# Fewer, longer scratch reads for the query features, and three moves in the order of work, in an attention-plus-GLU kernel

## The chip, the cores and the metric

The kernel runs on one core of a Trainium2 chip. The metric is the device time of one execution in microseconds (us), the median over several runs. Before the change it is 329.64 us (329.25 to 329.85 in 3 runs). The profile is one execution of the same kernel; its span is 327.9 us.

## What is computed

The inputs are q, k and v of shape (4 batches, 4 heads, 1088 positions, 32), two sketch matrices S1 and S2 of 8 x 32, and three feed-forward weights.

```python
def phi(x):                       # 32 numbers -> 64 features
    a = einsum('rd,bhsd->bhsr', S1, x)      # 8 numbers
    b = einsum('rd,bhsd->bhsr', S2, x)      # 8 numbers
    return outer(a, b)                      # 8 x 8 = 64
kv  = sum over s of phi(k) x v              # 64 x 32 per head
z   = sum over s of phi(k)                  # 64 per head
x   = (phi(q) @ kv) / (phi(q) @ z + 1e-6)   # heads side by side: (4352, 128)
out = (sigmoid(x @ w_gate) * (x @ w_val)) @ w_out    # d_ff = 1536
```

Everything is fp32. The weights arrive as 64-bit numbers whose halves the kernel puts together itself ("narrowing").

## The kernel before

**The feed-forward part is cut into waves.** The 4352 tokens are taken in chunks of 512, and the 1536 hidden columns in 12 blocks of 128. One wave (`w1`, L286) is one block of one chunk: two matmuls into a PSUM tile called wave (gate and value, L295), a sigmoid on ScalarE (sg, L303), and a gating multiply on VectorE (g, L313). The multiply is not emitted at once: `w1` leaves it in `moe["gate"]`, and `glu()` (L322) emits it when the next wave is due. The output matmul for the block (moeout, L255) follows one or two waves later. An fp32 matmul of the program shows as two PE records, so a wave is four records of L295 and two of L255. The wave tiles rotate through two PSUM buffers, which `qcomp` uses as well.

**During the first chunk the weights are still being narrowed.** Each wave of chunk 0 also emits one step each for several blocks (L304 to L308): two VectorE operations (L105, L109), a ScalarE square (L113), a GpSimd add (L114) and a last VectorE operation (L117) that writes the block of w_sb. A wave cannot start before the L117 of its own block.

**The attention part is worked batch by batch between the waves.** The order on TensorE, VectorE, ScalarE and GpSimd is written out by hand: `slot(group, n)` (L327) emits a group of attention work and then n waves. Instructions of one engine run strictly in the order in which they are emitted. Only the SyncE queue, which issues most DMAs, is ordered by the scheduler.

For a batch b: `turn_k` and `turn_q` (L353, L363) transpose k and q on VectorE. `kps` (L376) makes the sketches of k on TensorE and transposes them back on VectorE (kab, L391); `outer` (L397) makes phi(k) on GpSimd; `kv` (L519) sums over positions.

phi(q) is needed in another layout: 64 features on partitions, once for each of two position sets c, and all heads along the free axis. For batches 1 to 3 and for the second half of batch 0 it is built through DRAM. `qcomp` (L455) makes the compact sketches a and b and copies them to SBUF (cq). `spread` (L482) writes cq to a DRAM scratch tile dq and reads it back twice: into QP with each of the 8 rows of a repeated 8 times in place, and into BQ with the 8 rows of b cycled 8 times. `qmult` (L512) multiplies the two on VectorE (L515). Then `den` (L588) and `num` (L621) are the two products of phi(q) on TensorE, `invert` and `divide` finish x on VectorE.

The positions of a batch are in two halves n: `q_chk` gives 8 and 9 blocks of 32, that is 256 and 288 columns for each c. In the scratch tile before, `[c, h, i, r, column]`, one head's row r is 544 columns long (2,176 bytes), so a read covers one head, one c and one of a/b: 4 x 2 x 2 = 16 reads for each call of `spread`. In batch 0 only the second half goes this way (the first is computed directly, L679 to L692); there the 16 reads have rows of 288 columns, 1,152 bytes.

**The order around the change.** After the first wave of chunk 0 (L708), batch 0 goes on with

```python
    slot(q01, 6)                       # qcomp and spread of batch 0's second half, 6 waves
    qmult(0, 1)                        # VectorE, waits for all 16 reads
    slot(lambda: den(0, 1)(), 1)       # TensorE, reads what qmult wrote
    slot(lambda: num(0, 1)(), 1)
    turn_k(1)
    slot(None, 1)
    turn_q(1, 0)
    turn_q(1, 1)
    slot(None, 1)
```

and then each batch from 1 on starts with `begin(b)` (L711): kps, qcomp, spread, outer. When `begin` is called, the gating multiply of the last wave is still pending, so it is emitted after the kab transposes.

Of the kernel before, what the change touches and what calls it, by code (L numbers as in the profile page):

```python
# [8 lines left out]
F32 = mybir.dt.float32  # L9
# [5 lines left out]
MUL = ALU.mult  # L15

P = 128
# [3 lines left out]
def kernel(  # L21
# [12 lines left out]
    nc = tc.nc  # L34

    B, H, S, D = q.shape
    R = S1.shape[0]
# [359 lines left out]
    def outer(b, pi, m0, m1, j0=0, j1=NJK, eng=nc.gpsimd):  # L397
# [8 lines left out]
            op=MUL,  # L406
        )

    def ab(a_of=None, b_of=None, pool_b=None):

        mm = []
        if a_of is not None:
            aps = psm.tile([P, 2, 512], F32, tag="wave", name="aps")
            mm.append((a_of, aps, sa))
        if b_of is not None:
            pool, tag = (ps2, "two") if pool_b is None else pool_b
            bps = pool.tile([P, 2, 512], F32, tag=tag, name="bps")
# [14 lines left out]
        if a_of is not None:  # L432
            w = 32 * q_chk[a_of[2]][1]
            ASB[a_of] = sbA.tile([P, 2, 256], F32, tag="asb", name="asb", bufs=2)
            nc.scalar.copy(out=ASB[a_of][:, :, :w], in_=aps[:, :, :w])
        if b_of is not None:

            def mult():
                bb, pr, n = b_of
                if bb not in QP:  # L440
                    QP[bb] = sbA.tile([P, H, TP * 32], F32, tag="qp", name="qp")
                t0, tn = q_chk[n]
                w = 32 * tn
                nc.vector.tensor_tensor(
                    out=QP[bb][:, 2 * pr : 2 * pr + 2, 32 * t0 : 32 * t0 + w],
                    in0=bps[:, :, :w],
                    in1=ASB[b_of][:, :, :w],
                    op=MUL,
                )

            return mult
# [3 lines left out]
    def qcomp(b, ns, pool):  # L455
        t = pool[0].tile([P, 2, 512], F32, tag=pool[1], name="cqps")
        cq = sbA.tile([P, 2, 288], F32, tag="cq", name="cq", bufs=1)
        for c in range(2):
            for n in ns:
                t0, tn = q_chk[n]  # L460
                g = 2 * n + c
                for pi in range(2):
                    rows = slice(64 * pi, 64 * pi + 64)
                    nc.tensor.matmul(
                        out=t[32 * g : 32 * g + 32, pi, : 32 * tn],
                        lhsT=sk[rows, :],
                        rhs=qT_of[b][rows, t0 : t0 + tn, c, :],
                        start=True,
                        stop=True,
                    )  # L470
        w0, w1 = 32 * q_chk[0][1], 32 * q_chk[1][1]
        if 0 in ns:
            nc.scalar.copy(out=cq[:, :, :w0], in_=t[:, :, :w0])
            nc.scalar.copy(out=cq[64:, :, w0:w1], in_=t[64:, :, w0:w1])
        else:
            nc.scalar.copy(out=cq[64:, :, :w1], in_=t[64:, :, :w1])
        if b not in QP:
            QP[b] = sbA.tile([P, H, TP * 32], F32, tag="qp", name="qp")
        BQ[b] = sbA.tile([P, H, TP * 32], F32, tag="bq", name="bq", bufs=1)
        return cq  # L480

    def spread(b, ns, cq):  # L482
        w = TP * 32
        d = dram.tile([2, H, 2, R, w], F32, tag="dq", name="dq")
        for c in range(2):
            for n in ns:
                t0, tn = q_chk[n]
                g = 2 * n + c
                d0 = d[c, 0, 0, 0, 32 * t0 : 32 * t0 + 32 * tn]
                nc.sync.dma_start(  # L490
                    out=bass.AP(
                        tensor=d0.tensor,
                        offset=d0.offset,
                        ap=[[w, 4 * R], [4 * R * w, 2], [1, 32 * tn]],
                    ),
                    in_=cq[32 * g : 32 * g + 32, :, : 32 * tn],
                )
        w0, w1 = 32 * q_chk[ns[0]][0], 32 * sum(q_chk[ns[-1]])
        for h in range(H):
            for c in range(2):  # L500
                for i, (t, rows) in enumerate(
                    ((QP[b], [[w, R], [0, R]]), (BQ[b], [[0, R], [w, R]]))
                ):
                    d0 = d[c, h, i, 0, w0:w1]
                    nc.sync.dma_start(  # L505
                        out=t[64 * c : 64 * c + 64, h, w0:w1],
                        in_=bass.AP(
                            tensor=d0.tensor, offset=d0.offset, ap=rows + [[1, w1 - w0]]
                        ),
                    )  # L510

    def qmult(b, n):  # L512
        t0, tn = q_chk[n]
        cols = slice(32 * t0, 32 * t0 + 32 * tn)
        nc.vector.tensor_tensor(  # L515
            out=QP[b][:, :, cols], in0=QP[b][:, :, cols], in1=BQ[b][:, :, cols], op=MUL
        )

    def kv(b, j_list, zsum=None):  # L519

# [67 lines left out]
    def den(b, n):  # L588
        t0, tn = q_chk[n]
        w = 32 * tn  # L590
        dps = ps1.tile([P, 512], F32, tag="one", name="dps")
        for h in range(H):
            nc.tensor.matmul(  # L593
                out=dps[32 * h : 32 * h + 32, :w],
                lhsT=zb[b % 2][:, h, :],
                rhs=QP[b][:, h, 32 * t0 : 32 * t0 + w],
                start=True,
                stop=True,
            )

        def invert():

            dT = sbA.tile([P, 9, 32], F32, tag="dT", name="dT")
            nc.vector.transpose(out=dT[:, :tn].rearrange("p t c -> p (t c)"), in_=dps[:, :w])
            rc = sbA.tile([P, 9, 2], F32, tag="rc", name="rc")
            nc.vector.tensor_scalar_add(rc[:, :tn], dT[:, :tn, :2], 1e-6)
            nc.vector.reciprocal(out=rc[:, :tn], in_=rc[:, :tn])

            rb = sbA.tile([P, 9, 2, 32], F32, tag="rb", name="rb")
            r0 = rc[:, :tn]  # L610
            nc.vector.transpose(
                out=rb[:, :tn].rearrange("p t c s -> p (t c s)"),
                in_=bass.AP(
                    tensor=r0.tensor, offset=r0.offset, ap=[list(r0.ap[0]), [1, 2 * tn], [0, 32]]
                ),
            )
            RB[b, n] = rb

        return invert

    def num(b, n):  # L621
        t0, tn = q_chk[n]
        w = 32 * tn
        nps = ps2.tile([P, 2, 512], F32, tag="two", name="nps")
        for h in range(H):
            for c in range(2):
                rows = slice(64 * c, 64 * c + 64)
                nc.tensor.matmul(  # L628
                    out=nps[32 * h : 32 * h + 32, c, :w],
                    lhsT=ND[b][rows, 32 * h : 32 * h + 32],  # L630
                    rhs=QP[b][rows, h, 32 * t0 : 32 * t0 + w],
                    start=True,
                    stop=True,
                )
# [12 lines left out]

    steps = narrow(sr, sr_in, nc.vector) if wide else iter(())
    for _ in range(3):
# [13 lines left out]
        ),  # L663
        op=MUL,
    )
    sk = sk.rearrange("p m n r -> p (m n r)")
    sab = []
    for n, inner in enumerate(([[1, R], [0, R]], [[0, R], [1, R]])):
# [40 lines left out]
    cq = {}  # L709

    def begin(b):  # L711
        kps(b)
        cq[b] = qcomp(b, (0, 1), (psm, "wave"))
        spread(b, (0, 1), cq[b])
        for pi in range(2):
            for m in range(2):
                outer(b, pi, m, m + 1)
# [7 lines left out]
    def q01():  # L725
        spread(0, (1,), qcomp(0, (1,), (ps2, "two")))

    slot(q01, 6)
    qmult(0, 1)
    slot(lambda: den(0, 1)(), 1)  # L730
    slot(lambda: num(0, 1)(), 1)
    turn_k(1)
    slot(None, 1)
    turn_q(1, 0)
    turn_q(1, 1)
    slot(None, 1)
    for b in range(1, B):
        wn = 2 if b == 1 else 3
        load_batch(b + 1)
# [46 lines left out]
```

## Time and profile before

| | busy us | share of the span |
|---|---|---|
| TensorE matmul (PE) | 307.3 | 94% |
| VectorE (DVE) | 140.1 | 43% |
| ScalarE (ACT) | 81.4 | 25% |
| GpSimd (POOL) | 48.6 | 15% |

| group | count | busy us |
|---|---|---|
| wave matmuls, L295 | 432 | 194.2 |
| moeout matmuls, L255 | 216 | 106.6 |
| gating multiply g, L313 | 102 | 69.9 |
| qmult, L515 | 7 | 9.1 |

The DMA engines move 22.92 MB, 70 GB/s on average over the span, from 31,314 packets, of which 25,408 are under 2 KB. There are 64 reads of the scratch (qp<-dq and bq<-dq, 32 each).

How to read it: PE is busy nearly all the time, but "busy" counts a matmul at half clock as well as one at full clock. So the time that TensorE loses is in two places: stretches in which it does nothing, and stretches in which its granted clock (PEclk) is below 1.

### The profile page before, as it was taken

Reading aid. Unit: us, or ns where it says so; the run is one execution under the profiler, and the core shown is the slowest. Engines: PE = TensorE matmul, PEld = TensorE weight load, DVE = VectorE, ACT = ScalarE, POOL = GpSimd, SP = SyncE. Lnnn points to the kernel's source line nnn. Section 1 sums busy time; section 2 is a strip of 40 time slices with the busy share of each in tenths; the row PEclk is TensorE's granted clock in tenths of the full one; section 3 lists DMA queues with packets and bytes.
Section 4 is the critical chain, followed back from the end, with each engine's and each line's share of the span. In section 5 each row is a group of like instructions: output and inputs, shape, how many; then the busy total and the mean of one; then the engine's idle time right before and its main releaser. Section 6 shows DMA issues by size and latency. Waiting matters only on the chain.

```text
span 327.9 us, 3718 instructions
## 1 busy us (share of the span) xinstructions
PE 307.3 (94%) x1394; PEld 137.5 (42%) x1394; DVE 140.1 (43%) x241; ACT 81.4 (25%) x149; POOL 48.6 (15%) x57
## 2 busy tenths in 40 slices
PE   8789649996999899999999999999999999999994
PEld 2423214343433344444343444444444444444683
DVE  4887738631346513335544323455233222322331
ACT  2544503321121322121222221222222222222220
POOL 1435402570000190000003800000000000000000
PEclk9999959999699999999999999999999999999999
DMA  7997460547100145101001450010002000100021
GB/s 183 363 319 225 117 167 1 173 143 203 33 0 0 26 126 136 54 1 31 1 2 30 139 169 2 1 22 12 0 0 32 0 2 0 32 0 0 0 34 17
DMA packets 31314, 22.92 MB, mean 70 GB/s; under 512 B 19904, under 2 KB 25408, under 8 KB 31296
## 3 DMA queue, kind: packets, MB, share of 16 engines
q1 hardware_dynamic: 30464, 22.29, 24.5%
q10 hardware_dynamic: 832, 0.39, 0.6%
q8 instruction: 11, 0.18, 0.2%
q14 instruction: 7, 0.06, 0.1%
HBM read 19.46 MB, written 3.21 MB: 69 GB/s over the span
## 4 chain that ended last, share of the span: by engine, by line
PE 79%; DMA 6%; SPq 6%; DVE 5%; issue 1%; POOL 1%; ACT 1%; ACTq 0%; DVEq 0%; POOLq 0%
PE wave L295 48%; PE moeout L255 25%; SPq L505 6%; DMA dq<-cq 2%; PE dps L593 2%; DMA out_dram<-o_sb 1%; PE nps L628 1%; PE kvz L528 1%; DMA k<-in_k_dram 1%; PE kps L381 1%; DMA bq<-dq 1%; POOL head L114 1%; DVE w_sb L117 1%; DVE qp L515 1%; DVE kab L391 1%
## 5 line engine op out<-in xcount | busy, mean ns | idle before, releaser
L295 PE MATMUL wave<-xT,w_sb 128*128 128x512 f32 (+1 forms) x432 | 194.2, 577 | 2.2 <-DVE g L313 1.1
L313 DVE TENSOR_TENSOR g<-wave,sg 128x512 f32<-128x512 f32 x102 | 69.9, 686 | 129.0 <-ACT sg L303 128.9
L295 PEld LDWEIGHTS wave<-xT,w_sb 128*128 128x128 f32 x432 | 82.2, 192 | 101.2 <-issue 87.1
L303 ACT ACTIVATE sg<-wave 128x512 f32<-128x512 f32 x102 | 60.9, 597 | 217.4 <-PE wave L295 217.4
L255 PE MATMUL moeout<-g,w_sb 128*128 128x512 f32 (+1 forms) x216 | 106.6, 587 | 3.0 <-DVE g L313 3.0
L255 PEld LDWEIGHTS moeout<-g,w_sb 128*128 128x128 f32 x216 | 39.7, 193 | 47.4 <-issue 37.7
L402 POOL TENSOR_TENSOR kp<-kab 128x576 f32<-128x576 f32 x12 | 13.7, 1178 | 97.9 <-DVE kab L391 97.9
L114 POOL TENSOR_TENSOR head<-head,tail 128x384 int32<-128x384 int32 (+1 forms) x13 | 12.3, 946 | 31.6 <-DVE head L109 28.6
L515 DVE TENSOR_TENSOR qp<-qp,bq 128x1152 f32<-128x1152 f32 (+1 forms) x7 | 9.1, 1296 | 13.3 <-DMA out_dram<-o_sb 7.5
L593 PE MATMUL dps<-qp,zb 128*32 128x256 f32 (+1 forms) x64 | 6.1, 436 | 8.0 <-DVE qp L515 7.6
L638 DVE TENSOR_TENSOR xT<-nps,rb 128x512 f32<-128x512 f32 (+1 forms) x8 | 5.8, 725 | 14.1 <-PE nps L628 13.9
L117 DVE SCALAR_TENSOR_TENSOR w_sb<-cap,head 128x384 f32<-128x384 f32 x12 | 9.2, 767 | 4.5 <-POOL head L114 4.5
L113 ACT ACTIVATE cap<-cap 128x384 f32<-128x384 f32 (+1 forms) x13 | 6.5, 501 | 8.5 <-DVE head L109 8.5
L228 PE MATMUL warm<-ones 128*128 128x512 f32 (+1 forms) x10 | 7.2, 858 | 1.0 <-DVE hm L234 1.0
L97 POOL TENSOR_SCALAR cap<-w_in 128x384 f32<-128x384 f32 x12 | 6.6, 558 | 7.7 <-DMA w_in<-in_moe_w_out_dram 7.7
L562 POOL TENSOR_TENSOR z<-kp 128x1024 f32<-128x1024 f32 x3 | 7.1, 2364 | 0.2
L109 DVE SCALAR_TENSOR_TENSOR head<-cap,head 128x384 int32<-128x384 int32 (+1 forms) x13 | 6.9, 533 | 0.4
L593 PEld LDWEIGHTS dps<-qp,zb 128*32 128x32 f32 x64 | 1.6, 111 | 12.7 <-DVE qp L515 8.5
L101 ACT ACTIVATE tail<-w_in 128x384 int32<-128x384 uint32 x12 | 6.5, 554 | 1.5 <-DMA w_in<-in_moe_w_out_dram 1.5
L528 PE MATMUL kvz<-kp,v 128*32 128x64 f32 (+1 forms) x288 | 6.7, 222 | 0.1
L628 PE MATMUL nps<-qp,nd 64*32 64x256 f32 (+1 forms) x128 | 6.1, 401 | 0.7 <-issue 0.7
L528 PEld LDWEIGHTS kvz<-kp,v 128*32 128x32 f32 (+1 forms) x288 | 5.3, 109 | 3.5 <-issue 2.7
(55 smaller groups left out, 87.7 us busy)
## 6 DMA issues: line engine op xcount, KB each, us to landing
qp<-dq SPq DMA_DIRECT2D x24, 136.0 KB
bq<-dq SPq DMA_DIRECT2D x24, 136.0 KB
v<-in_v_dram SPq DMA_DIRECT2D x16, 144.0 KB
k<-in_k_dram SPq DMA_DIRECT2D x3, 544.0 KB
q<-in_q_dram SPq DMA_DIRECT2D x3, 544.0 KB
w_in<-in_moe_w_gate_dram SPq DMA_DIRECT2D x6, 256.0 KB
w_in<-in_moe_w_val_dram SPq DMA_DIRECT2D x6, 256.0 KB
w_in<-in_moe_w_out_dram SPq DMA_DIRECT2D x6, 256.0 KB
```

Of the source, the lines that this page charges most:

```text
L114: nc.gpsimd.tensor_tensor(out=head, in0=head, in1=tail, op=ALU.add)
L117: nc.vector.scalar_tensor_tensor(out=out, in0=cap.bitcast(F32), scalar=1.265625 * 2.0**-30, in1=head.bitcast(F32), op0=ALU.is_ge, op1=MUL,)
L255: nc.tensor.matmul(out=moe["acc"][:, :tw], lhsT=w_sb[:, 2, j, :], rhs=g[:, jj, :tw], start=(j == 0), stop=(j == NJ - 1),)
L295: nc.tensor.matmul(out=wv[:, which, jj * tw : (jj + 1) * tw], lhsT=w_sb[:, which, j0 + jj, :], rhs=xT[:, t0 : t0 + tw], start=True, stop=True,
L303: nc.scalar.activation(out=sg, in_=wv[:, 0], func=ACTF.Sigmoid)
L313: nc.vector.tensor_tensor(out=g, in0=wv[:, 1], in1=sg, op=MUL)
L402: eng.tensor_tensor(out=o0.rearrange("p j m (i l) -> p (j m) i l", i=R), in0=bass.AP(tensor=a0.tensor, offset=a0.offset, ap=[pst] + jm + [ ...
L505: nc.sync.dma_start(out=t[64 * c : 64 * c + 64, h, w0:w1], in_=bass.AP(tensor=d0.tensor, offset=d0.offset, ap=rows + [[1, w1 - w0]]),)
L515: nc.vector.tensor_tensor(out=QP[b][:, :, cols], in0=QP[b][:, :, cols], in1=BQ[b][:, :, cols], op=MUL)
L528: nc.tensor.matmul(out=kvz[32 * h : 32 * h + 32, F * which : F * which + F], lhsT=v_t[b][:kr, h, j, :] if which == 0 else ones[:kr, :], rh ...
L593: nc.tensor.matmul(out=dps[32 * h : 32 * h + 32, :w], lhsT=zb[b % 2][:, h, :], rhs=QP[b][:, h, 32 * t0 : 32 * t0 + w], start=True, stop=True,)
L628: nc.tensor.matmul(out=nps[32 * h : 32 * h + 32, c, :w], lhsT=ND[b][rows, 32 * h : 32 * h + 32], rhs=QP[b][rows, h, 32 * t0 : 32 * t0 + w] ...
```

## The change

Three things are changed.

1. **The scratch layout and its reads.** The scratch tile is now one for each half n, with the order `[c, i, r, h, column]`: the four heads lie next to each other, so one row is 4 x 256 or 4 x 288 columns (4,096 or 4,608 bytes). QP and BQ are laid out alike, half by half, each half with the heads side by side (`half`). One read then covers one half, one c and one of a/b for all heads: 2 x 2 = 4 reads for a half, 8 for a batch with both halves, where the kernel before has 16 for a call (read half by half and head by head it would be 32). The half that is multiplied first is also written and read first. For this the rows of cq must come out in another order, so the query sketches use a reordered copy of the weights, skq, which one small GpSimd copy makes at the start. The heads lie in the order 0, 2, 1, 3, which `den` and `num` look up.
2. **Gating ahead of kab.** `begin` calls `glu()` first, so the pending gating multiply stands ahead of the kab transposes on VectorE.
3. **Batch 0's product one wave later.** `qmult(0, 1)` now stands after 7 waves of the loop instead of 6, and the transposes of batch 1's k and q are moved ahead of it. Batch 1 then begins after 10 waves instead of 11.

```diff
+    def half(t, n):
+        t0, tn = q_chk[n]
+        o, w = 32 * H * t0, 32 * tn
+        return t[:, o : o + H * w].rearrange("p (h w) -> p h w", h=H)
...
-                        lhsT=sk[rows, :],
+                        lhsT=skq[rows, :],
...
     def spread(b, ns, cq):
-        w = TP * 32
-        d = dram.tile([2, H, 2, R, w], F32, tag="dq", name="dq")
-        for c in range(2):
-            for n in ns:
-                t0, tn = q_chk[n]
+        for n in ns:
+            w = 32 * q_chk[n][1]
+            d = dram.tile([2, 2, R, H, w], F32, tag=f"dq{n}", name="dq")
+            for c in range(2):
                 g = 2 * n + c
...
                 nc.sync.dma_start(
...
+                    out=d[c].rearrange("i r (m p) w -> (i r m) p w", m=2),
+                    in_=cq[32 * g : 32 * g + 32, :, :w],
                 )
-        for h in range(H):
-            for c in range(2):
-                for i, (t, rows) in enumerate(
-                    ((QP[b], [[w, R], [0, R]]), (BQ[b], [[0, R], [w, R]]))
-                ):
-                    d0 = d[c, h, i, 0, w0:w1]
+            for i, t in enumerate((QP[b], BQ[b])):
+                for c in range(2):
+                    d0 = d[c, i]
+                    rows = [[H * w, R], [0, R]] if i == 0 else [[0, R], [H * w, R]]
                     nc.sync.dma_start(
-                        out=t[64 * c : 64 * c + 64, h, w0:w1],
+                        out=half(t, n)[64 * c : 64 * c + 64].rearrange("p h w -> p (h w)"),
                         in_=bass.AP(
-                            tensor=d0.tensor, offset=d0.offset, ap=rows + [[1, w1 - w0]]
+                            tensor=d0.tensor, offset=d0.offset, ap=rows + [[1, H * w]]
                         ),
                     )
...
-                rhs=QP[b][:, h, 32 * t0 : 32 * t0 + w],
+                rhs=half(QP[b], n)[:, 2 * (h % 2) + h // 2, :],
...
+    skq = const.tile([P, 2, R, 2], F32, tag="skq")
+    nc.gpsimd.tensor_copy(out=skq, in_=sk.rearrange("p m n r -> p n r m"))
+    skq = skq.rearrange("p n r m -> p (n r m)")
...
     def begin(b):
+        glu()
         kps(b)
...
-    slot(q01, 6)
+    slot(q01, 4)
+    turn_k(1)
+    slot(None, 2)
+    turn_q(1, 0)
+    turn_q(1, 1)
+    slot(None, 1)
     qmult(0, 1)
     slot(lambda: den(0, 1)(), 1)
     slot(lambda: num(0, 1)(), 1)
-    turn_k(1)
-    slot(None, 1)
-    turn_q(1, 0)
-    turn_q(1, 1)
-    slot(None, 1)
```

More of the change, by code (lines that the diff above doesn't have):

```diff
@@ L440, in mult @@
                 if bb not in QP:
[L441 removed]
+                    QP[bb] = sbA.tile([P, H * TP * 32], F32, tag="qp", name="qp")
                 t0, tn = q_chk[n]
@@ L444, in mult @@
                 nc.vector.tensor_tensor(
-                    out=QP[bb][:, 2 * pr : 2 * pr + 2, 32 * t0 : 32 * t0 + w],
+                    out=half(QP[bb], n).rearrange("p (m c) w -> p c m w", m=2)[:, pr],
                     in0=bps[:, :, :w],
@@ L477, in qcomp @@
         if b not in QP:
-            QP[b] = sbA.tile([P, H, TP * 32], F32, tag="qp", name="qp")
-        BQ[b] = sbA.tile([P, H, TP * 32], F32, tag="bq", name="bq", bufs=1)
+            QP[b] = sbA.tile([P, H * TP * 32], F32, tag="qp", name="qp")
+        BQ[b] = sbA.tile([P, H * TP * 32], F32, tag="bq", name="bq", bufs=1)
         return cq
     def spread(b, ns, cq):
-        w = TP * 32
-        d = dram.tile([2, H, 2, R, w], F32, tag="dq", name="dq")
-        for c in range(2):
-            for n in ns:
-                t0, tn = q_chk[n]
+        for n in ns:
+            w = 32 * q_chk[n][1]
+            d = dram.tile([2, 2, R, H, w], F32, tag=f"dq{n}", name="dq")
+            for c in range(2):
                 g = 2 * n + c
-                d0 = d[c, 0, 0, 0, 32 * t0 : 32 * t0 + 32 * tn]
                 nc.sync.dma_start(
[L491 to L496, printed above, removed]
-                )
-        w0, w1 = 32 * q_chk[ns[0]][0], 32 * sum(q_chk[ns[-1]])
-        for h in range(H):
-            for c in range(2):
-                for i, (t, rows) in enumerate(
-                    ((QP[b], [[w, R], [0, R]]), (BQ[b], [[0, R], [w, R]]))
-                ):
-                    d0 = d[c, h, i, 0, w0:w1]
+                    out=d[c].rearrange("i r (m p) w -> (i r m) p w", m=2),
+                    in_=cq[32 * g : 32 * g + 32, :, :w],
+                )
+            for i, t in enumerate((QP[b], BQ[b])):
+                for c in range(2):
+                    d0 = d[c, i]
+                    rows = [[H * w, R], [0, R]] if i == 0 else [[0, R], [H * w, R]]
                     nc.sync.dma_start(
-                        out=t[64 * c : 64 * c + 64, h, w0:w1],
+                        out=half(t, n)[64 * c : 64 * c + 64].rearrange("p h w -> p (h w)"),
                         in_=bass.AP(
-                            tensor=d0.tensor, offset=d0.offset, ap=rows + [[1, w1 - w0]]
+                            tensor=d0.tensor, offset=d0.offset, ap=rows + [[1, H * w]]
                         ),
@@ L512, in qmult @@
     def qmult(b, n):
[L513 to L517, printed above, removed]
+        q0 = half(QP[b], n)
+        nc.vector.tensor_tensor(out=q0, in0=q0, in1=half(BQ[b], n), op=MUL)
     def kv(b, j_list, zsum=None):
@@ L630, in num @@
                     lhsT=ND[b][rows, 32 * h : 32 * h + 32],
-                    rhs=QP[b][rows, h, 32 * t0 : 32 * t0 + w],
+                    rhs=half(QP[b], n)[rows, 2 * (h % 2) + h // 2, :],
                     start=True,
```

## The prediction

> **What bounds the kernel now.** First the page: the busy and clock rows in 40 slices of 8.2 us.
>
> ```profile
> PE   8789649996999899999999999999999999999994
> PEclk9999959999699999999999999999999999999999
> ```
>
> TensorE is full except at the start, in the fifth and sixth slice (33 to 49 us) and in the tenth (74 to 82 us), and the granted clock drops in the sixth and the eleventh. The matmuls themselves stay, so only those two holes can be won or lost. The waits of TensorE say who made them (total us, times, longest):
>
> ```profile
> PE dps L593 <- DVE qp L515: 7.6, 1, 7.6
> PE moeout L255 <- DVE g L313: 3.0, 1, 3.0
> PE wave L295 <- DVE g L313: 1.1, 1, 1.1
> ```
>
> The timeline of the first hole, start and duration in us:
>
> ```profile
> 31.37 0.69 SPq L505 DMA_DIRECT2D qp<-dq  x1
> ...
> 36.27 1.98 PE L295 MATMUL wave<-xT,w_sb 128*128 128x512 f32 x4
> ...
> 39.47 0.56 DVE L109 SCALAR_TENSOR_TENSOR head<-cap,head 128x384 int32<-128x384 int32 x1
> ...
> 40.86 0.57 SPq L505 DMA_DIRECT2D bq<-dq  x1
> ...
> 44.48 1.36 DVE L515 TENSOR_TENSOR qp<-qp,bq 128x1152 f32<-128x1152 f32 x1 [4.46 <-DMA bq<-dq]
> 45.89 1.49 PE L593 MATMUL dps<-qp,zb 128*32 128x288 f32 x8 [7.63 <-DVE qp L515]
> ```
>
> TensorE ends its seventh wave at 38.26 and idles to 45.89. VectorE had finished the narrowing at 40.03 and waited 4.46 us for the last of 16 reads. They are issued one by one, 0.62 us apart (31.37 to 40.86); the last landed 3.6 us after its issue. Even with the data there, the product could not have begun before 40.03, so 3.1 us of the hole (38.26 to 40.03, and 1.36) are VectorE's.
>
> The second hole, 79.23 to 82.25, is `qmult(1, 0)`: VectorE was free at 72.86, the product began at 80.37, and the gating multiply behind it released TensorE. Its wait is booked to an output DMA, but that does not feed it; what it needs are the scratch reads, issued until 75.5. TensorE ran on for 6.4 us (72.86 to 79.23) before it felt this.
>
> Last, the clock, cut into stretches of 3.41 us (length, PE busy and instructions, clock, DMA share, GB/s):
>
> ```profile
> 37.11:40.52 3.41, 1.15 (x3) 1.00 0.44 121
> 40.52:43.93 3.41, 0.00 (x0) 0.50 0.60 196
> 43.93:47.35 3.42, 1.46 (x9) 0.50 0.93 221
> 47.35:50.76 3.41, 3.41 (x5) 0.50 0.01 1
> 78.07:81.48 3.41, 1.16 (x3) 1.00 0.72 169
> 81.48:84.90 3.42, 2.65 (x3) 0.50 0.49 122
> 84.90:88.31 3.41, 3.41 (x7) 0.50 0.00 0
> ```
>
> A stretch that is one third busy is followed by half clock, and one that is 2.65/3.41 busy does not lift it; a full one does. So the holes also cost (50.76 - 45.89)/2 = 2.4 us and (88.31 - 82.25)/2 = 3.0 us.
>
> [...]both drops lie on one grid, 12 x 3.41 us apart.[...] The reads have 64 partitions on one side and 8 scratch rows on the other[...]; while batch 2's reads drain alone, the DMA share is half:
>
> ```profile
> 124.00:126.00 2.00, 2.00 (x6) 0.91 (x5) 0.60 (x1) 0.60 (x1) 0.00 (x0) 1.00 0.53 143
> ```
>
> (last columns: clock, DMA share, GB/s.) In the changed kernel the dimensions are 64 and 8 again, so I keep 8 engines.
>
> **The change part by part.**
>
> *The reads.* Batch 0's half is the same 64 x 16 x 1,152 B = 1.18 MB in 4 reads. Issue: 4 x 0.62 = 2.5 us instead of 16 x 0.62 = 9.9, from 31.37 on, since what stands ahead of it in the queue stays. Then the transfer decides. The trace of before has no 4 KB row on 8 engines, so I bound it: 141 GB/s (row above, 2,176-byte rows) gives 8.4 us; the 97 GB/s of the slowest stretch in which reads ran (31 to 33, half filled) gives 12.2; the 194 GB/s of 74 to 76 gives 6.1. I take 8.4 and 1.5 us for the start: landed at 31.4 + 1.5 + 8.4 = 41.3 (range 39 to 45).
>
> *The product one wave later.* Waves are counted from 0, so the one at 36.27 is wave 6. The order on VectorE is now: narrowing steps emitted with wave 4, transpose of k (1.30), g, L117, ..., narrowing steps of wave 6, two transposes of q (1.36), g, L117, L105, L109, product. All of this is behind one another, and TensorE's next step is the product's reader. Step by step, with durations of before:
>
> - L109 at 33.58, k transpose 34.06 to 35.36, g to 35.98, L117 to 36.5 (it no longer overlaps GpSimd's L97, so 0.54 as at 49.72, not 0.88). Wave 6 starts at 36.5 instead of 36.27.
> - L105, L109 to 37.3, GpSimd L114 37.5 to 38.5, L117 38.5 to 39.4: wave 7 starts at 39.45 and ends at 41.4.
> - L105, L109 to 40.3, q transposes to 41.6, g to 42.2, L117 to 42.7, L105, L109 to 43.5, product 43.5 to 44.85.
>
> The data, at 41.3, are there before 43.5: the wait on DMA is gone, but VectorE's own queue takes its place. TensorE idles 41.4 to 44.85, 3.45 us instead of 7.63, and one wave more is done. On the grid above, 40.52 to 43.93 is busy for 0.9 us: half clock from 43.93, and 43.93 to 47.35 is busy for 2.5, less than the 2.65 that did not suffice, so full clock returns at 50.76 as before. Until then, before did (50.76 - 45.89)/2 = 2.43 us of full-clock work, now (50.76 - 44.85)/2 = 2.95 plus a wave with its output product of 6 x 0.43 = 2.58. **Gain: 2.95 + 2.58 - 2.43 = 3.1 us.**
>
> Batch 1 then begins two waves after the product instead of four, at about 54.7 instead of 60.34. The transposes moved out from between those waves cost nothing there; TensorE had no gap at 55 to 60.
>
> *Batch 1's reads.* Scratch writes go out 1.9 us after the begin, reads 4.75 us after it as before (60.34 to 65.09): at 59.4. The first half, needed first, is 64 x 4 x 4,096 B = 1.05 MB: 7.4 us at 141 GB/s (5.4 to 10.8), landed at about 68.3 (66 to 72). VectorE reaches the product 12.5 us after the begin (60.34 to 72.86), at 67.2, and TensorE feels it 6.4 us later, at 73.6. So the second hole closes in the whole range. **Gain: 3.0 + 3.0 = 6.0 us.** The second half, another 8.4 us, lands near 77 and is needed three waves (7.7 us) and the sum over positions (1.5) later than the first, at 76.5 on VectorE, again with several us until TensorE feels it. Batches 2 and 3 had no such hole and have more waves between.
>
> *Gating ahead of kab.* At each begin the next wave but one needs the buffer that this gating multiply frees. In batch 2 it ran at 113.45 behind kab (0.85); its sigmoid was done at 112.57. TensorE was free at 113.06 and started at 114.16. With g first, 112.57 to 113.26, wave start about 113.3; and since the chunks are shifted by one wave, an output product lies in between there and hides the rest. Gain 1.1 us; in batches 1 and 3 the same wave started 0.3 and 0.4 us after the product ahead of it could have ended (62.34 to 62.65, 177.98 to 178.36). **Gain: 1.8 us.** The price is kab 0.6 us later, so GpSimd's features of k too; they are read by the sums at 134.96, over 10 us after GpSimd ended, and in batch 1 (GpSimd ends at 71.7, sums at 74.86) 3.1 us are left. Nothing.
>
> *At nothing:* skq, one GpSimd copy of 128x32 (the 128x64 add took 0.32 us), while GpSimd idles 7.7 us before 12.08; first used at 20.5. The products on contiguous halves: [...]the trace has 1,152 columns in 1.35 us, so I leave it. Matmul operands of the same size, in other places: nothing. The loads of q, v and k for later batches leave the queue earlier, behind the reads, and are needed after 95 us.
>
> Sum: 329.64 - 3.1 - 6.0 - 1.8 = 318.7.
>
> **The rivals.**
>
> *The clock does not drop in the first hole.* With another phase the 3.45 us fall half into each of two windows, and both are half busy. Speaks for: the hole is about as long as a window. Against: the grid is the same over the whole trace and three runs agree within 0.6 us. Gain of a further 2.95: 315.8.
>
> *The reads are bound by eight engines at the low rate*, 12.2 us: data at 45.1, product 1.6 us later than 43.5, and the clock with it: 320.5. If they are later still, the first hole is as long as it was but one wave later; the second stays shut to 73.6: up to 322.
>
> *The second hole stays in part*, because the sums of k or another producer wait there instead: half of its 6 us back, 321.7, all of it 324.7.
>
> *Slower.* Long rows, each read eight times over by engines in step, might run at 50 GB/s. Batch 0's data land at 31.4 + 1.5 + 23.6 = 56.5, 13 us after 43.5; batch 1's first half takes 21 us, lands 13.7 later than at 141 GB/s, 8 past the 73.6; with 3 more for the clock and 2 in later batches 318.7 + 13 + 8 + 3 + 2 = 345. For it: the rate fell from 194 to 141 GB/s between batches 1 and 2 with no change of shape. Against: rows of 2 KB and more elsewhere move over 360 GB/s on 16 engines.
>
> **How the numbers follow.** The forecast 0.66, no drop of the clock 0.12, low rate 0.11, part of the second hole 0.06, slower 0.05. The two steps of the first hole are good to a us or so each, since they chain fifteen durations. The range goes from the second case, 315.3, to the third, 322.0. Faster 0.94, the same 0.01, slower 0.05.
>
> **What would show it.** Right: TensorE's longest wait is for L515 of batch 0 and is 3 to 4 us, with VectorE's product starting without a wait on a DMA; half clock in one stretch only, about 44 to 51 us; begin of batch 1 at 54 to 55; no wait of TensorE for g near 75 us, nor behind kab; the reads' DMA share near 0.5. Wrong: a product that waits for bq<-dq, a DMA share near 0.5 at under 100 GB/s, or a new wait of VectorE between the transposes and the product.

## The result and the profile after

| | median us | runs | ratio to before, 95% interval |
|---|---|---|---|
| before | 329.44 | 328.33 to 329.85 (4) | |
| changed | 320.11 | 318.24 to 321.76 (4) | 0.972 [0.9661, 0.9779] |

The change saves 9.3 us; the prediction had 10.9. A later comparison (label e9_after below) gave a median of 321.14 against 330.41, which is again 9.3 us, and a ratio of 0.9763 [0.9694, 0.9833], which is 7.8. A median here is over all executions, while a ratio compares only those within 1.5% of the fastest of their kernel, so the two can differ. Executions of one kernel differ by several us, so one profile is read below for its mechanism, and the medians and ratios for the size. The profiled execution of the changed kernel took 321.76 us, the longest of its four.

The page of the changed kernel, busy and clock rows in 40 slices of 8.0 us, and then its waits of TensorE (total us, times, longest):

```profile
PE   8789919999899999999999999999999999999995
PEclk9999986999999999999999999999999999999999
```
```profile
PE dps L587 <- DVE qp L511: 7.6, 1, 7.6
PE moeout L255 <- DVE g L313: 1.6, 2, 0.9
```

The second hole is gone from the busy row, with its drop of the clock. The wait of a wave for g is gone from the waits. But the first hole, which was to shrink to 3.45 us, is as long as it was: 7.6 us. The timeline of the changed kernel says why (start, duration in us; what ended the idle time before in brackets):

```profile
30.84 1.40 SPq L502 DMA_DIRECT2D qp<-dq  x2
...
32.28 1.20 SPq L502 DMA_DIRECT2D bq<-dq  x2
...
33.59 0.39 SPq L177 DMA_DIRECT2D q<-in_q_dram  x1
...
34.02 2.80 SPq L191 DMA_DIRECT2D v<-in_v_dram  x4
...
38.98 1.88 PE L295 MATMUL wave<-xT,w_sb 128*128 128x512 f32 x4
...
42.29 0.56 DVE L109 SCALAR_TENSOR_TENSOR head<-cap,head 128x384 int32<-128x384 int32 x1
...
47.04 1.36 DVE L511 TENSOR_TENSOR qp<-qp,bq 128x1152 f32<-128x1152 f32 x1 [4.19 <-DMA bq<-dq]
48.45 1.19 PE L587 MATMUL dps<-qp,zb 128*32 128x288 f32 x8 [7.59 <-DVE qp L511]
...
57.43 0.72 PE L381 MATMUL kps<-kT,sk 64*32 64x288 f32 x16
```

The four reads are issued in 2.6 us (costed 2.5). VectorE is done with the narrowing at 42.85 (42.29 + 0.56; costed 43.5). But the product begins at 47.04, when bq arrives, 5.7 us after the 41.3 of the prediction. Between the reads and the product stand the loads of q and v for batch 2, and from 40.49 on a load of k for batch 3. In the kernel before, the queue was still issuing scratch reads at 41. The same stretch in windows of the changed kernel (last columns: clock, DMA share, GB/s):

```profile
37.00:39.00 2.00, 2.00 (x6) 0.74 (x6) 1.39 (x3) 0.88 (x3) 1.38 (x2) 1.00 1.00 216
39.00:41.00 2.00, 1.86 (x5) 0.55 (x4) 1.97 (x5) 0.99 (x3) 1.16 (x2) 1.00 1.11 164
41.00:43.00 2.00, 0.00 (x0) 0.00 (x0) 1.81 (x4) 1.11 (x3) 0.33 (x1) 1.00 1.11 168
```

The share of the 16 DMA engines is 1.00 to 1.11 here, where the reads alone had 0.53 (batch 2 of the kernel before); and they move only 164 to 216 GB/s, for the reads and the loads together. The trace's records of single packets tell the two apart: the reads' 256 packets of 4,608 bytes (no other transfer here has this size) run from 32.27 to 45.81, which is 87 GB/s, and the product begins 1.2 us after the last of them.

The second hole, timeline of the changed kernel:

```profile
82.01 1.36 DVE L511 TENSOR_TENSOR qp<-qp,bq 128x1152 f32<-128x1152 f32 x1 [2.08 <-DMA bq<-dq]
```
```profile
85.60 1.13 PE L255 MATMUL moeout<-g,w_sb 128*128 128x512 f32 x2 [0.89 <-DVE g L313]
```

VectorE still waits for batch 1's data, at 72.90 for the first half (2.41 us) and at 82.01 for the second, but TensorE feels only 0.89 us of it, and the clock stays up.

Where the time came from is seen by stage. The starts of kps (L381) in the timeline are the begins of batches 1, 2 and 3:

| | begin(1) | 1 to 2 | 2 to 3 | 3 to the end | span |
|---|---|---|---|---|---|
| before | 60.34 | 51.52 | 64.13 | 151.9 | 327.9 |
| changed | 57.43 | 46.09 | 62.95 | 153.5 | 320.0 |

Batch 1 begins after one wave fewer, which with its output product is 2.58 us and comes back in the last stage. So the first stage gained 60.34 - 57.43 - 2.58 = 0.3 us, the second 5.4, the third 1.2, the last 151.9 + 2.58 - 153.5 = 1.0: together the 7.9 us between the two spans. A few tenths of such a difference say little: the first read of batch 0 leaves at 31.37 in the trace of before and at 30.84 in this one.

### The profile page after: what moved, and what is told of

It reads as the page before. It is cut to its first block, busy times and chain, and to the rows that moved or that the text cites. A ratio compares the mean times of both kernels' runs of the same rounds, so it can differ in the third digit from the quotient of the medians.

```text
span 320.0 us, 3677 instructions
## 1 busy us (share of the span) xinstructions
PE 302.6 (95%) x1394; PEld 136.2 (43%) x1394; DVE 140.7 (44%) x241; ACT 81.5 (25%) x149; POOL 49.3 (15%) x58
## 4 chain that ended last, share of the span: by engine, by line
PE 77%; DMA 12%; SPq 4%; DVE 3%; issue 1%; POOL 1%; ACT 0%; POOLq 0%; DVEq 0%
PE wave L295 47%; PE moeout L255 25%; DMA bq<-dq 9%; SPq L502 2%; DMA w_in<-in_moe_w_out_dram 2%; PE nps L622 2%; PE dps L587 2%; DMA dq<-cq 1%; DVE qp L511 1%; PE kvz L522 1%; POOL head L114 1%; SPq L494 1%; PE kps L381 1%; SPq L191 1%; DVE w_sb L117 1%
## 5 line engine op out<-in xcount | busy, mean ns | idle before, releaser
L295 PE MATMUL wave<-xT,w_sb 128*128 128x512 f32 (+1 forms) x432 | 192.0, 572 | 0.8 <-DVE w_sb L117 0.4
L632 DVE TENSOR_TENSOR xT<-nps,rb 128x512 f32<-128x512 f32 (+1 forms) x8 | 5.8, 724 | 13.4 <-PE nps L622 13.3
L265 DVE STREAM_TRANSPOSE o_sb<-moeout 128x512 f32<-128x512 f32 (+1 forms) x9 | 6.1, 678 | 1.4 <-PE moeout L255 1.3
```

The costliest lines, as they stand in the source:

```text
L295: nc.tensor.matmul(out=wv[:, which, jj * tw : (jj + 1) * tw], lhsT=w_sb[:, which, j0 + jj, :], rhs=xT[:, t0 : t0 + tw], start=True, stop=True,
```

## Experiments: each part alone

These three apply one part of the change to the kernel before. They ran beside one another, beside e4_hold and beside the kernel before, whose median was 329.09 us. Of the later experiments, e5_hold_den, e6_hold_qp16 and e8_hold_v ran in a second comparison (before: 330.06), e7_den, e9_after and e10_hold in a third (330.41).

**e1_layout**: part 1 only (scratch layout, 8 reads, skq).

```diff
-        d = dram.tile([2, H, 2, R, w], F32, tag="dq", name="dq")
+            d = dram.tile([2, 2, R, H, w], F32, tag=f"dq{n}", name="dq")
... (reads, half(), skq as in the change; the order of work as before)
```

> Only the scratch layout and its eight reads are new; order of batch 0 and gating as before. Two theories on why batch 0's four reads landed 14 us after the last was issued (32.9 to 47.0) in the changed kernel. Contention: the loads of q, v and k of later batches, which now stand right behind the reads, share engines and HBM with them; then here, where k of batch 3 still waits for the later transpose, the reads land at about 44 and the first hole is as before, so 329.4 - 5 (second hole) = about 324.5. Shape: long rows read eight times over are slow by themselves (80 GB/s); then they land at 47 again, the first hole grows by 2.5 us and the time is about 327.

326.05 us, ratio 0.9913 [0.9883, 0.9943]: between the two expectations. Its waits of TensorE:

```profile
PE dps L587 <- DVE qp L511: 8.4, 1, 8.4
PE moeout L255 <- DVE g L313: 2.3, 1, 2.3
```

With a quarter of the issues the first hole is not shorter but longer. The product began at 44.96 after a wait of 5.19 us on bq<-dq; in the kernel before, with the last read issued at 40.86, it began at 44.48. The loads of q and v left the queue at 33.60 and 34.03, straight behind the reads.

The second hole gave 2.0 us and not 5 (begins at 60.16 and 109.65). The product of batch 1's first half began 16.6 us after the begin instead of 20.0, and TensorE no longer felt it. But the second half's product began 26.3 us after the begin (86.49), and now TensorE stood 2.33 us for that one, with half clock for one stretch of 3.41 us after it: 6.0 - 2.3 - 1.7 = 2.0.

**e2_order**: part 3 only, on the old layout with 16 reads a call.

```diff
-    slot(q01, 6)
-    qmult(0, 1)
-    slot(lambda: den(0, 1)(), 1)
-    slot(lambda: num(0, 1)(), 1)
+    slot(q01, 4)
     turn_k(1)
-    slot(None, 1)
+    slot(None, 2)
     turn_q(1, 0)
     turn_q(1, 1)
     slot(None, 1)
+    qmult(0, 1)
+    slot(lambda: den(0, 1)(), 1)
+    slot(lambda: num(0, 1)(), 1)
```

> Old layout with 16 reads; only batch 0's product comes one wave later with the transposes ahead of it. Both theories: the reads are issued one by one until 41 and land at 44, product at 44.5 with one wave more done, so 3.1 us less in the first hole; the second hole stays (16 reads of batch 1 are issued over 10 us). About 326.3.

322.54 us, ratio 0.9807 [0.976, 0.9855]: 6.5 us, twice what I had expected, and the largest of the three parts. Its timeline:

```profile
44.31 1.36 DVE L515 TENSOR_TENSOR qp<-qp,bq 128x1152 f32<-128x1152 f32 x1 [1.36 <-DMA q<-in_q_dram]
...
45.72 1.49 PE L593 MATMUL dps<-qp,zb 128*32 128x288 f32 x8 [4.75 <-DVE qp L515]
```

Sixteen reads, the last issued at 40.47, feed the product at 44.31: earlier than four reads do in the changed kernel (47.04). (The product's wait is booked to a load of q, which does not feed it.) The loads of q and v could not leave before 41.14, since the reads stood ahead of them. By stage (begins at 55.49, 103.92, 167.18; span 321.6) it gains 2.3 in the first, 3.1 in the second, 0.9 in the third. In the second, 2.9 us of hole were still there but no drop of the clock came with it, so these 3.1 us are the half clock of before and not the hole. In this trace an edge between two stretches of the clock falls into the hole, at 75.40, and leaves each of them partly busy (2.39 and 1.52 of 3.41 us); the mean clock of all six executions is 0.989, as in the profiled one, and why none of them dropped here stays open. In the third, the wait for g behind kab is gone although g was not moved, because an output product now stands in between. So part of what the gating was to bring came with the order already.

**e3_gate**: part 2 only.

```diff
     def begin(b):
+        glu()
         kps(b)
```

> Old layout and order; only the gating multiply ahead of kab. Both theories: the waits of TensorE for g at the three begins go (1.8 us): about 327.6. The first and second holes stay as before.

327.28 us, ratio 0.9978 [0.9952, 1.0005]: 1.8 us in the medians, but only 0.7 by the ratio, whose interval reaches 1, so a gain in time is not shown. In its trace the waits of waves for g are 0.3 us instead of 1.1, and the stage from begin(2) to begin(3) is 0.8 us shorter (173.71 - 110.40 = 63.31).

By the medians the parts save 3.0 + 6.5 + 1.8 = 11.3 us and the whole 9.3; by the ratios 2.9 + 6.4 + 0.7 = 10.0 and 9.2, each good to 1 or 2 us. So the times do not show whether the parts overlap. The traces do in one place: in the stage from begin(2) to begin(3) gating alone gained 0.8 us and the order alone 0.9, the whole change 1.2. With the layout the first hole did not shrink, alone (begin(1) at 60.16 instead of 60.34) or in the whole change.

## Experiments: the loads behind the reads

Theory: the loads of q, v and k slow the reads down although they stand behind them in the queue, because they use the DMA engines, or what lies behind these, at the same time. Rival: rows of 4,608 bytes read eight times over are slow by themselves.

**e4_hold**: the changed kernel, with a one-element memset on VectorE into each tile that a load of batches 2 and 3 fills. The memsets stand behind batch 0's product and behind batch 1's second one, so those loads cannot leave earlier. This also moves the load of k of batch 2, which in the changed kernel leaves at 27.5, ahead of the reads; but its last packet ends at 32.62 there, as the first ones of the reads run (32.27), so it explains little.

```diff
             t = ld.tile([P, T, D], F32, tag=tag, name=tag)
+            if b >= 2:
+                nc.vector.memset(t[:, :1, :1], 0.0)
...
     qmult(0, 1)
+    load_batch(2)
...
-        load_batch(b + 1)
...
         qmult(b, 1)
+        load_batch(b + 2)
```

> The changed kernel, but the loads of batches 2 and 3 are held back until batch 0's product (for batch 2) and batch 1's second product (for batch 3) have run on VectorE, by a one-element write into each tile there. Contention theory: batch 0's reads run alone, at the 140 GB/s of the later batches, and land near 41; VectorE reaches the product at 42.9 without a wait, TensorE idles 3.4 us instead of 7.6: about 316. Shape theory: they land at 47 as before, 320.

317.61 us, ratio 0.9655 [0.9608, 0.9702]. Its windows, with the same columns as above:

```profile
37.00:39.00 2.00, 2.00 (x6) 0.90 (x5) 1.40 (x3) 0.59 (x2) 1.49 (x2) 1.00 0.50 129
39.00:41.00 2.00, 2.00 (x6) 0.71 (x4) 1.97 (x5) 1.50 (x3) 0.63 (x1) 1.00 0.45 118
41.00:43.00 2.00, 0.40 (x1) 0.00 (x0) 1.97 (x5) 1.04 (x2) 0.87 (x2) 1.00 0.02 6
```

The same long rows, read alone, use half of the engines (shares of 0.50 and 0.45) at 118 to 129 GB/s and are through at 41 (last packet at 41.29; the prediction had 41.3). The product began at 43.30 without a wait, and TensorE's hole was 3.30 us. The rival falls.

**e9_after and e10_hold**: since the gain over the changed kernel (2.5 us) came from two comparisons with overlapping intervals, the changed kernel and e4_hold's kernel ran once more, side by side.

> The changed kernel itself, beside the two below on one chip. Profile runs so far give 318.2 to 321.8 us; if the phase of the clock grid spreads the runs, its median here is 319 to 320.5 and its profile shows the product of batch 0 at 47 us behind bq<-dq.

> The changed kernel with the loads of batches 2 and 3 held until the scratch reads have landed. If these loads delay the reads, 2 to 3 us less than the changed kernel on the same chip (316.5 to 318); if the earlier difference was chance, the same time within 0.5 us.

321.14 us (0.9763 [0.9694, 0.9833]) and 318.51 us (0.969 [0.9622, 0.9758]), beside 330.41 for the kernel before. The difference of the medians is 2.6 us, about as the first time. The intervals of the ratios overlap again; the two times six executions themselves give a difference of means of 2.4 us with a 95% interval of about 0.5 to 4.3, so that there is a gain is shown, its size hardly. In e9_after's trace the product began at 46.48, behind bq<-dq. e10_hold's timeline:

```profile
43.46 1.36 DVE L515 TENSOR_TENSOR qp<-qp,bq 128x1152 f32<-128x1152 f32 x1
...
44.87 1.19 PE L591 MATMUL dps<-qp,zb 128*32 128x288 f32 x8 [3.52 <-DVE v L192]
...
54.72 0.71 PE L385 MATMUL kps<-kT,sk 64*32 64x288 f32 x16
```

Product at 43.46 (predicted 43.5), hole 3.52 (3.45; it is booked to the memset that follows the product), begin(1) at 54.72 (54.7). With the loads out of the way the prediction's chain for the first hole comes out to a tenth of a us; that half clock followed the hole as in the forecast is luck in part, as e4_hold shows. The gain there is 60.34 - 54.72 - 2.58 = 3.0 us.

This pair of traces does not show the 2.6 us of the medians, though. e10_hold's profiled execution took 319.86 us and e9_after's 319.32: it begins batch 1 1.5 us earlier, but needs 46.91 us to the next begin where e9_after needs 44.93. There VectorE waits 2.21 and 2.87 us for batch 1's two halves instead of 1.38 and 0. So a part of what the hold wins in the first hole can be lost again behind it.

**e8_hold_v**: which loads matter? Only v of batch 2 is held; q of batch 2 and k of batch 3 go behind the reads.

```diff
-            v_t[b] = load_v(b)
+            if b != 2:
+                v_t[b] = load_v(b)
...
     qmult(0, 1)
+    v_t[2] = load_v(2)
```

> The changed kernel with only v of batch 2 held back until batch 0's product; q of batch 2 and k of batch 3 (1.1 MB in rows of 4.3 KB) stand right behind the reads. If any load behind the reads slows them by its bytes, the reads land near 45, as with q and v behind them in e1_layout, and the time is about 319. If it is v's short rows (1,152 bytes, 32 partitions each), they land near 41 and the time is about 317.6, as in e4_hold.

318.52 us, ratio 0.9659 [0.9615, 0.9703], no different from e4_hold's 0.9655, so the time does not decide. Its timeline:

```profile
44.20 1.36 DVE L514 TENSOR_TENSOR qp<-qp,bq 128x1152 f32<-128x1152 f32 x1 [1.15 <-DMA bq<-dq]
```

With q and k behind the reads (1.1 MB) the product could begin at 44.2, with q and v (1.15 MB, e1_layout) at 45.0, with all three (1.7 MB) at 47.0 and 46.5. From first to last packet the reads took 10.7, 11.7, and 13.5 and 13.4 us, and 9.4 and 9.8 with nothing behind them (e4_hold, e10_hold). So v's short rows are not needed for a delay. That the delay goes by the bytes alone is not shown by one trace of each, and e7_den below does not fit it.

**e6_hold_qp16**: is the DMA share of half a matter of the eight source rows? e4_hold's kernel with the rows of a stored twice, so that a qp read has 16 source rows (bq still 8), at the price of four more small writes a batch.

```diff
-            d = dram.tile([2, 2, R, H, w], F32, tag=f"dq{n}", name="dq")
+            da = dram.tile([2, R, 2, H, w], F32, tag=f"da{n}", name="da")
+            db = dram.tile([2, R, H, w], F32, tag=f"db{n}", name="db")
...
-                    rows = [[H * w, R], [0, R]] if i == 0 else [[0, R], [H * w, R]]
+                    rows = [[H * w, 2 * R], [0, R // 2]] if i == 0 else [[0, R], [H * w, R]]
```

> As e4_hold, but the rows of a are stored twice in the scratch, so that the source of the qp reads has 16 rows[...]; the bq reads keep 8. If the number of engines sets the rate, the DMA share goes above 0.5 while qp is read, the reads of batch 1 drain about a quarter sooner and VectorE's two waits of 2.4 us for batch 1's halves shrink: about 1 us less than e4_hold. If the repeated rows in HBM set it, the drain and the time stay as in e4_hold or get worse by the extra writes.

318.27 us, ratio 0.9646 [0.9608, 0.9685], no gain over e4_hold (0.9655). Its windows:

```profile
32.00:34.00 2.00, 1.89 (x5) 0.65 (x5) 1.59 (x3) 1.04 (x2) 0.84 (x2) 1.00 0.78 235
36.00:38.00 2.00, 2.00 (x5) 1.03 (x6) 1.81 (x4) 0.97 (x2) 0.58 (x1) 1.00 0.56 127
```

While the qp reads run, share and rate rise to 0.78 and 235 GB/s; with only bq left they fall back to 0.56 and 127. The reads of batch 0 were through two us earlier (38.6), but there VectorE decides anyway. In batch 1 the reads left later, with more writes ahead of them: the first 6.1 us behind the begin instead of 4.4, those of the second half 15.5 instead of 7.0. The two products began 15.1 and 25.1 us behind the begin, in e4_hold 15.4 and 24.9, so nothing was gained.

## Experiments: another wave in the hole

What is left of the first hole once the data are there is VectorE's own work (transposes, narrowing, product) between TensorE's last wave and den. Another wave can stand there.

**e7_den** (on the changed kernel) and **e5_hold_den** (on e4_hold's): one more `slot` ahead of den.

```diff
     qmult(0, 1)
+    slot(None, 1)
     slot(lambda: den(0, 1)(), 1)
```

> As e4_hold, and batch 0's den one wave later than its product on VectorE, so that TensorE has a wave to do while VectorE makes the product. If the 3.3 us hole of e4_hold is VectorE's own queue (transposes, narrowing, product), it shrinks to under 1 us: about 314 (3.3 us less, and no half clock after it). If the product were still waiting on a DMA, it would stay near 317.6.

> The changed kernel, loads not held, with one more wave between batch 0's product and its reader. The wave (2.1 us and its output product) fills part of the hole of 7.6 us, so about 5 us stay and the begin of batch 1 comes no later: 2.6 us less than the changed kernel, 317.5. If the loads behind the reads are what matters, it stays 1.5 to 2.5 us above the version with both (315.6). If instead a wave in the hole is all that is needed, 315.6 as well.

e5_hold_den: 315.55 us, ratio 0.9563 [0.953, 0.9595], the lowest ratio of all; 314 was expected. Its waits of TensorE:

```profile
PE moeout L259 <- DVE g L317: 4.0, 4, 2.3
```

No wait for qp is left; what remains is batch 1's products, which hold a gating multiply back (VectorE waits there 8.0 us in all for bq<-dq).

e7_den: 318.07 us, ratio 0.9672 [0.9591, 0.9753]. The median is 3.1 us below the changed kernel beside it and 2.5 above e5_hold_den, near what was expected. But its runs are wide (314.28 to 321.59), its interval overlaps that of the changed kernel and just touches that of e5_hold_den, which ran in another comparison; so neither difference is shown by it. And its profiled execution, the fastest of the six, did not do what I expected of it. The product began at 43.18 without a wait, with the q, v and k loads behind the reads as in the changed kernel. Its windows:

```profile
37.00:39.00 2.00, 2.00 (x6) 0.78 (x5) 1.40 (x3) 0.72 (x2) 1.49 (x2) 1.00 0.98 287
39.00:41.00 2.00, 2.00 (x6) 0.71 (x4) 1.97 (x5) 1.39 (x3) 0.74 (x1) 1.00 1.10 232
```

At shares of 0.98 and 1.10 the engines moved 287 and 232 GB/s here, where the changed kernel had 216 and 164 and e9_after 186 and 126, up to 41 us with the same transfers. So the loads behind the reads do not cost a fixed amount. Here the reads took 9.2 us from first to last packet, as if alone; in the traces of e8_hold_v, e1_layout, e9_after and the changed kernel they took 10.7 to 13.5.

The packets also say what the delay is not. Added up, the time of the reads' packets fills 6.9 to 7.9 engines in all these traces, which speaks against the loads taking the reads' turns on their engines. What changes is the time of one packet: 0.27 to 0.30 us in e4_hold, e5_hold_den and e10_hold, 0.27 here, and 0.33 to 0.41 in the four delayed traces. The loads slow each packet down, in some executions and not in others. What it is that they share (HBM, the fabric, the writes into SBUF) I did not settle.

## Why the prediction was right or wrong

**The time** was 320.1 (then 321.1) against 318.7. One step of the first hole failed, one of the second was mis-sized, and it is luck in part that the total came this close: the two traces of the changed kernel gained 0.3 and 1.6 us in the first stage instead of 3.1, 5.4 and 6.6 in the second instead of 6.3, and 1.0 in the last, where 0.4 was forecast and the rest is unexplained. (The range began at 315.3, though the case named for this end sums to 315.8.)

**The step that failed** is the last of "at nothing": "The loads of q, v and k for later batches leave the queue earlier, behind the reads, and are needed after 95 us." I asked when they are needed, and not what they take from the transfer ahead of them. Fewer issues end the queue's work 8 us earlier (q's load leaves at 33.59 instead of 41.53), and the queue uses that to send 1.7 MB more into the stretch in which the reads drain (on 6.9 of 16 engines by their packets). The product could begin at 47.0 instead of 43.5, behind bq<-dq, which the prediction itself had named as a sign of being wrong; the first hole gave 0.3 us in that trace (1.6 in e9_after, with begin(1) at 56.19). Being ahead in the queue did not protect the reads: a packet of theirs took 0.37 us on average in this trace, and 0.27 to 0.30 with the loads held. Of my rivals "bound by eight engines at the low rate" had nearly this time (320.5 to 322), and the reads did run at 87 and 88 GB/s in the two traces of the changed kernel. But the mechanism is another one, which e4_hold shows: alone, still at a DMA share of about half (0.45 to 0.53 from 33 to 41 us), the reads ran at 121 to 129 GB/s by their packets (e4_hold, e5_hold_den, e10_hold), not far from the 141 that I had taken (the row that I took it from shows 143). The 1.5 us for the start was an estimate; the first packet ran at 32.27, 1.4 us after the first issue (30.84, changed kernel). With the us or so from the last packet to the product the data are usable at about 42.3 to 43.4 even then (an estimate from these traces) rather than at 41.3; the 43.5 at which VectorE is ready just covers that.

**The rest of the first hole** (VectorE at 43.5, hole 3.45, begin at 54.7) was right, as e10_hold shows.

**The second hole** closed: the stage from begin(1) to begin(2) gained 5.4 us in the profiled run and 6.6 in e9_after (101.12 - 56.19 = 44.93), against 6.0 and 0.3 for gating. But the prediction gave the 6.0 to the reads, and the reads alone (e1_layout) gained 2.0 there; the order alone, with the old reads, gained 3.1, as half clock stayed away in e2_order. The first half came as argued. The term that was wrong is the second half, put at nothing: it came at 82.0 instead of 77 (2.7 us of this is the late begin, the rest a rate of 110 to 149 GB/s from 62 to 76 us, stores of the output among it, where I had 141), and the "several us until TensorE feels it" were 1.2: VectorE waited 2.08 us and TensorE 0.89. In e1_layout the same term cost 2.33 us and a stretch at half clock.

**Gating**: the stage from begin(2) to begin(3) gained 1.2 us, predicted 1.1, and the wait of the wave for g is gone. But gating alone gained 0.8 there (e3_gate) and the order alone 0.9, since the shift of one wave already puts a product ahead of the waiting wave (e2_order); beside it gating adds about 0.3. Of the 1.8 us forecast for all three begins the times of e3_gate show no gain clear of noise.

**Eight engines**: right as far as the share shows it, 0.45 to 0.53 of 16 for reads alone (e4_hold, e10_hold). That it would stay so in the new layout was an estimate from the 0.53 of the kernel before, whose reads had 8 source rows too; with 16 source rows for qp, e6_hold_qp16 showed 0.78. The 50 GB/s of the slower case was a guess and was not shown: even with the loads behind them batch 0's reads ran at 87 and 88 GB/s (changed kernel, e9_after).

**The clock**: half clock followed in the changed kernel, but there after a hole of 7.6 us; the forecast hole of 3.45 us came only with the loads held, and then the clock dropped in e10_hold and not in e4_hold. The argument against its absence, "the grid is the same over the whole trace and three runs agree", was wrong. e4_hold and e10_hold are one kernel with holes of 3.30 and 3.52 us; the first kept full clock and began batch 1 at 51.52, the second at 54.72, and 3.0 us of that are half clock (9.85 us from den to the begin instead of 6.82). Counted from the start of the span, the grid lies elsewhere in each trace: an edge is at 44.32 in e10_hold and at 43.32 in e4_hold, 1.00 us apart, where one stretch is 3.41. Three runs were too few to show the spread: the 43 executions of the kernel before beside e1_layout lie between 324.98 and 332.94 us, and they follow their mean granted clock: the seven at 0.986 or more took 324.98 to 327.43 us, the nine at 0.973 or less 329.77 to 332.94.

## What to carry to other kernels

When a change makes a queue's issues fewer, ask what the queue will send next and whether that runs at the same time as the transfer that is waited for: that it stands behind it in the queue was no protection here (0.33 to 0.41 us for a packet of the reads in four traces, 0.27 to 0.30 with the loads held; only in e7_den did it stay at 0.27 with the loads behind). Such loads can be held until the critical data have landed, for instance with a one-element write into their tile behind the consumer; here that was worth 2.6 us in the medians. And put independent TensorE work between a VectorE product and the matmul that reads it, rather than only making its data come sooner: TensorE's hole ahead of den, 3.30 us in e4_hold, was gone with it in e5_hold_den, and the ratio was 0.9563 instead of 0.9655.

## What the runs showed of the hardware

- Reads with 8 source rows, each repeated 8 times, drained on a DMA share of about 0.5, with rows of 4,608 bytes at 118 to 143 GB/s (e4_hold and e10_hold, windows from 33 to 41), with the 2,176 of the kernel before at 143 (batch 2) and up to 194 (batch 1, 74 to 76); 16 source rows for half of the reads gave 0.78 and 235 GB/s.
- With loads behind them the DMA share was 0.98 to 1.11 from 37 to 41 us (changed kernel, e9_after, e7_den), but the total was anything from 126 to 287 GB/s; a packet of the reads took 0.27 to 0.41 us, alone 0.27 to 0.30.
- Where the product waited for these reads, it began 0.9 to 1.2 us after their last packet (e8_hold_v, e1_layout, e9_after, changed kernel).
- The gating multiply whose sigmoid ended at 75.57 in the kernel before ran at 81.51, behind the product that stood ahead of it on VectorE and waited until 80.37.
- The clock record of the kernel before shows full and half clock in turn, for 34.133, 10.240, 30.720, 6.827 and 238.933 us, that of the changed kernel for 40.960, 6.827 and 266.240 (each without the half clock of its last 3 us): 10, 3, 9, 2 and 70 times, and 12, 2 and 78 times 3.4133 us. The stretches of 3.41 us lie differently in these traces: the drop came at 40.52 before, at 46.14 after, at 44.32 in e10_hold, and not at all in e4_hold. Where the edges of the stretches are known, the rows are (changed kernel, then e10_hold, then e4_hold, whose edges follow from its next drop, at 312.97, 79 times 3.4133 us after 43.32):

```profile
39.32:42.73 3.41, 1.54 (x4) 0.38 (x2) 3.38 (x7) 1.67 (x4) 1.50 (x2) 1.00 1.09 156
42.73:46.14 3.41, 0.00 (x0) 0.00 (x0) 0.12 (x1) 0.52 (x1) 0.99 (x1) 1.00 1.01 203
46.14:49.55 3.41, 1.10 (x8) 0.20 (x8) 1.36 (x1) 0.00 (x0) 0.00 (x0) 0.50 0.78 193
```
```profile
40.91:44.32 3.41, 0.43 (x2) 0.00 (x0) 3.24 (x6) 1.56 (x3) 1.73 (x3) 1.00 0.17 42
44.32:47.73 3.41, 2.86 (x10) 1.04 (x11) 2.02 (x8) 0.00 (x0) 1.35 (x1) 0.50 0.47 126
```
```profile
39.90:43.32 3.42, 1.50 (x4) 0.38 (x2) 3.39 (x8) 1.64 (x4) 1.50 (x2) 1.00 0.14 36
43.32:46.73 3.41, 2.03 (x12) 0.84 (x13) 2.52 (x9) 0.52 (x1) 1.95 (x1) 1.00 0.28 64
```

Stretches busy for 1.50 and 1.54 of 3.41 us kept full clock; stretches of 0.00 and 0.43 lost it, as the 1.15 of before did; one busy for 2.86 at half clock did not bring it back. In e4_hold an edge falls into the hole (41.40 to 44.70) and leaves both stretches partly busy; in e10_hold nearly the whole hole lies in one. So in these two traces a hole of 3.3 to 3.5 us cost the clock or not by where the edges fell.
